# Far-half residual sums stored with 32-column blocks exchanged, and the far operands of the up projection read in one 128-partition transfer each

## The chip, the cores and the metric

The kernel runs on one core of one Trainium2 chip. Its time is the device time of one execution in microseconds (us); a median is taken over several runs. A profiled execution, taken by the hardware profiler, gives each instruction's start and duration. The engines are PE (matrix multiplications), DVE (vector), ACT (activations), POOL (a second element-wise engine) and SP, which computes nothing here and issues nearly all the transfers (DMAs) between DRAM and the on-chip memory, one after the other in a fixed order.

## The reference

One transformer layer on a sequence of 2048 tokens of width 1024: a layer norm, linear attention with a learned feature map (32 heads of width 32), an output projection `wo` with a residual, a second layer norm, and a dense layer of width 3584 with a relu, with a second residual. All in float32.

```python
x = A_x
h = x + _A_ref(_layernorm(x, axis=-1), A_wqkv, A_w_phi, A_wo)
h2 = h + _B_ref(_layernorm(h, axis=-1), B_w1, B_w2)
# _A_ref: q, k, v = x @ wqkv; phi = [softmax(p), softmax(-p)] with p = q @ w_phi (k alike)
#         o = phi_q (phi_k^T v) / (phi_q sum(phi_k)); o @ wo
# _B_ref: relu(x @ w1) @ w2
```

## The kernel before

**Staging.** PE runs matrix products from beginning to end: keys and values, queries, attention, the output projection (wo), the up projection (w1) and the down projection (w2). Each float32 operand is split into a high part, rounded to the form that PE takes, and the low remainder, and every product is three matmuls: high x high, high x low, low x high (`mm3`, L181 to L184). For a weight, ACT makes the high part (L125), and DVE or POOL subtracts it for the low part (L129); the weight's raw form comes by an SP transfer (L337) into a ring of six tiles called raw.

**Tokens and products.** The 2048 tokens are sixteen tiles of 128. Tiles 0 to 7 are the near half (b=0), tiles 8 to 15 the far half (b=1). In the up and down projections the operands are cut into 2 x 2 blocks and multiplied by a fast scheme with seven block products, m=1 to 7, in place of eight. The order of the seven in the up projection is UP = (1, 5, 6, 2, 7, 3, 4), with two column groups p of the weight in turn for each m: the up projection runs over b, then over pairs of p, then over m, then over the two p. Each m has an operand tile hT (named hT1 to hT7) of 128 partitions x 2 parts (high, low) x 4 x 512. The near half's operands stand in these tiles from the start of the up projection; when m's last product of the near half has run, the far half's operand of that m is loaded over it.

**From wo to the operands.** `wo_load` (L656 to L658) reads half a row block of x into one of four tiles called xh (128 x 512). When PE has the wo product of that half block in PSUM, `wo_add` (L683, L684) adds it on DVE, in place, giving the residual sum h. `wo_store` (L686, L687) writes h to DRAM, to hd. For a far tile `far_stats` (L735 to L741) takes the layer norm's statistics from the same tile. During the up projection of the near half, `far_pair` (L756 to L786) reads hd of a far tile back into xin, normalizes it on ACT, transposes it in blocks of 32 x 32 on DVE (L754), and forms the seven sums of the block scheme; `far_store` (L789 to L794) writes these to DRAM, to hs[1, m]. Here a block of 32 columns of the model width stands on 32 partitions: the transposes of 32 x 32 blocks leave, of the four blocks a and the four blocks c that make up 512 columns, a in the partitions and c in the columns, where the operand wants c in the partitions and a in the columns.

**The operand's load.** `h_load` (L798 to L808) reads hs[b, m] into the low part of hT[m], in two halves g=0 and 1. For b=0 it is two transfers of 256 KB (L804). For b=1 it is four transfers (L808), one for each q, of 32 partitions by 4 x 256 columns, 128 KB each: in these the blocks a and c change places. Then ACT copies it into the high part (`h_high`, L816), and DVE subtracts (`h_low`, L820). PE's matmuls read both.

**Down.** `d_load` (L903 to L907) reads h from hd again, `d_add` (L909, L910) adds the down product in PSUM, and `d_store` (L912 to L915) writes the output. One name (x1 to x4) is one quarter of a half's output, and takes one or two products in turn: the first `d_add` of a name is that of the m which also loads it.

**Order.** Nothing is scheduled by dependencies alone. The program counts PE's steps: a step is three matmuls, an item of wo is eight steps, an item of the up projection four. `do` (L189) and `when` (L971) set each piece of work beside one step, and each engine executes its instructions in the order in which the program was recorded. The tables that matter here: L1109 to L1118 put the load of a wo item, its add (nine steps after the item's start, eleven for the first two) and its store (fourteen steps after); L1143 to L1154 put `h_load`, `h_high` and `h_low`. For b=1 the load of m stands at the step behind m's last near product plus 2j + 3g, with j its place in UP (0 to 6) and g its half; `h_high` 22 + 4g and `h_low` 25 + 4g steps behind the step with g=0. L1177 to L1187 do the same for the down projection.

**SP's queue.** SP issues in program order, and what stands behind a waiting transfer waits too. The built program gives SP's transfers eight completion counters in turn, so each SP transfer also waits until the eighth transfer before it has landed: at most eight are in flight.

Of the kernel before, what the change touches and what calls it, by code (L numbers as in the profile page):

```python
# [9 lines left out]
F32 = mybir.dt.float32  # L10
# [5 lines left out]
P = 128  # L16
# [6 lines left out]
HT = NT // 2  # L23
# [26 lines left out]
BANK_OF = {6: 1, 7: 1, 4: 1, 3: 5}  # L50
# [90 lines left out]
def kernel(  # L141
# [12 lines left out]
    v, act, pool, pe, sp = nc.vector, nc.scalar, nc.gpsimd, nc.tensor, nc.sync  # L154
# [18 lines left out]
    def f32(ap):  # L173
        return ap.bitcast(F32)
# [14 lines left out]
    def do(n, k, f, *args):  # L189
        at[n, k].append((f, args))  # L190
# [11 lines left out]
    hs = {(b, m): dram.tile([P, 4, 4, P], F32, name=f"hs{b}_{m}") for b in range(2) for m in UP}  # L202
# [448 lines left out]
            v.tensor_sub(at_out(u, 1, g), at_in(ps), f32(at_out(u, 0, g)))  # L651

    oT, opool = {}, {}
    xh, wo_ps = {}, {}

    def wo_load(t, hf):  # L656
        xh[t, hf] = hp.tile([P, 512], F32, name="xh", bufs=4)
        sp.dma_start(xh[t, hf], x[t * P:(t + 1) * P, hf * 512:(hf + 1) * 512])  # L658

    def wo_item(t, hf, keys):  # L660
        b, i = place_of[t]
        o = oT[b]
        ps = wo_ps[t, hf] = mm_bank()
        for c in range(8):
            w = W.get(keys[c])
            mm3(ps, o[:, 0, c, i * P:(i + 1) * P], o[:, 1, c, i * P:(i + 1) * P], w[:, 0, :], w[:, 1, :],
                c == 0, c == 7)
            yield
# [12 lines left out]
            yield  # L681

    def wo_add(t, hf):  # L683
        v.tensor_add(xh[t, hf], wo_ps.pop((t, hf)), xh[t, hf])  # L684

    def wo_store(t, hf):  # L686
        sp.dma_start(hd[t][:, hf * 512:(hf + 1) * 512], xh.pop((t, hf)))  # L687
# [108 lines left out]
    sums, hT = {}, {}  # L796

    def h_load(b, m, g):  # L798

        cols = slice(2 * g * P, 2 * (g + 1) * P)  # L800
        if b == 0:
            lo = hT[m][:, 1, :, cols].rearrange("p k (i n) -> p k i n", i=2)
            for i in range(2):
                sp.dma_start(f32(lo[:, :, i, :]), hs[b, m][:, 2 * g + i])  # L804
            return
        src = hs[b, m].rearrange("(a k) q i n -> q k a (i n)", a=4)
        for q in range(4):
            sp.dma_start(f32(hT[m][32 * q:32 * (q + 1), 1, :, cols]), src[q, :, :, cols])  # L808

    def h_parts(m, g):  # L810

# [74 lines left out]
    dbank = {}  # L886
# [14 lines left out]
    d = {}  # L901

    def d_load(b, name, q):  # L903

        r, hf = {"x1": (0, 0), "x2": (0, 1), "x3": (1, 0), "x4": (1, 1)}[name]
        d[name, q] = t = dp.tile([P, 512], F32, name=f"{name}_{q}")
        sp.dma_start(t, hd[HT * b + 4 * r + q][:, hf * 512:(hf + 1) * 512])  # L907

    def d_add(b, m, name, q):  # L909
        v.tensor_add(d[name, q], dbank[b, BANK_OF.get(m, m)][q], d[name, q])  # L910

    def d_store(b, name, q):  # L912
        r, hf = {"x1": (0, 0), "x2": (0, 1), "x3": (1, 0), "x4": (1, 1)}[name]
# [6 lines left out]
    def item(gen, *args, keys):  # L920
        items.append((gen, args + (keys,)))
        steps.extend((k,) for k in keys)
        return len(items) - 1
# [10 lines left out]
    wo_first = len(items)  # L934
    for b, tiles in enumerate(groups):
        for hf in range(2):

            pairs = b == 0 and hf == 0
            for j in range(0, 4, 2 if pairs else 1):
# [3 lines left out]
                for half in range(2):  # L943
                    n = item(wo_pair, tiles[j:j + 2], hf, half, keys=[("wo", hf, 4 * half + k // 2) for k in range(8)])
# [26 lines left out]
    def when(step, f, *args):  # L971

        if step < 8 * first_up:
            do(step // 8, step % 8, f, *args)
        else:
            do(first_up + (step - 8 * first_up) // 4, step % 4, f, *args)
# [4 lines left out]
    for t in range(1, NT):  # L981
        n = t - 1 if t < HT else q_n[1, t - HT] + 1
# [125 lines left out]

    order = sorted(wo_n.items(), key=lambda kv: kv[1])  # L1109
    for (t, hf), n in order:  # L1110
        do(max(n - 1, wo_first), -1, wo_load, t, hf)
        added = 8 * n + (11 if n < wo_first + 2 else 9)
        when(added, wo_add, t, hf)
        if t >= HT:
            when(added, far_stats, t, hf)
            if hf == 1:
                when(added + 4, ln_power, ("f", t))
        when(8 * n + (10 if n > order[-3][1] else 14), wo_store, t, hf)  # L1118
# [24 lines left out]
    for j, m in enumerate(UP):  # L1143

        for g in range(2):
            step = up0 + (8 * j + (-62, -32)[g] if j < 4 else 6 * (j - 4) + 10 + 2 * g)
            high = up0 + (8 * j + (-48, -19)[g] if j < 4 else 6 * (j - 4) + 20 + 2 * g)
            when(step, h_load, 0, m, g)
            when(high, h_high, m, g)
            when(high + (2 if j < 4 else 5), h_low, m, g)  # L1150
            step = up_step(0, NP - 1, m) + 2 * j
            when(step + 3 * g, h_load, 1, m, g)
            when(step + 22 + 4 * g, h_high, m, g)
            when(step + 25 + 4 * g, h_low, m, g)  # L1154
# [22 lines left out]
    for b in range(2):  # L1177
        for m in DOWN:
            n = down_n[b, m, NP - 1] + 1
            name, more = {1: "x1", 5: "x4", 6: "x2", 4: "x3"}.get(m), \  # L1180
                {3: "x2", 7: "x4", 2: "x1", 4: "x3"}.get(m)
            for q in range(4):
                if name:
                    do(n - 8, q, d_load, b, name, q)
                do(n, q, d_add, b, m, name or more, q)
                if more:
                    do(n + 1, q, d_store, b, more, q)  # L1187

# [101 lines left out]
```

## Time and profile before

| quantity | value |
|---|---|
| runs | 1884.54, 1890.76, 1887.76 us; median 1887.76 us |
| profiled execution, its own time | 1886.22 us |
| its span (first to last instruction) | 1884.4 us |
| mean granted PE clock in it | 0.998 of full speed |
| bytes moved by DMA | 432.17 MB, 229 GB/s over the span |
| SP transfers called raw<-t (256 KB each) | 224, median 4.0 us from issue to landing |
| SP transfers called ad<-c (256 KB each) | 112, median 3.7 us |
| statistics of a far tile, 128 x 512, on DVE (L738) | 0.694 us |

A row of a timeline is: start, duration, engine, line, operation, out <- in, count; in brackets the idle time just ahead of it and the work whose end released it. A row of a window is, for each engine, busy time and the number of instructions, then the granted PE clock, the busy share of the sixteen DMA engines, and what they moved in GB/s. The chain of waits is followed back from the last instruction: each piece is what the next one waited for. The names in it: raw<-t and raw<-in_w_dram are raw weights loaded, ad<-c and ad<-s are results of the up projection stored, hT<-hs is `h_load`. SPq stands for SP's issuing of a transfer, PEld for PE's loading of weights, which runs beside its matmuls.

### The profile page before, as it was taken

What the parts mean: (1) busy time and instruction counts of PE and PEld (TensorE: products, weight loads), DVE (VectorE), ACT (ScalarE), POOL (GpSimd) and SP (SyncE); (2) the same over time, 40 slices, a digit from 0 to 9 for tenths busy, and PEclk for the clock granted to TensorE, in tenths of its full rate; (3) what the DMA queues carried; (4) which work ended last, traced back from release to release, by engine and by line L of the source; (5) the groups of instructions that cost most, each with busy time, mean ns of one, the idle gap of its engine ahead of it and who ended that gap; (6) DMA issues with size and microseconds to landing.
All of it is one profiled execution on the core that took longest, in us unless ns stands there. A gap on an engine that the chain in (4) does not pass through costs nothing.

```text
span 1884.4 us, 31901 instructions
## 1 busy us (share of the span) xinstructions
PE 1872.2 (99%) x11608; PEld 1535.5 (81%) x11608; DVE 1069.7 (57%) x1695; ACT 739.2 (39%) x1271; POOL 973.2 (52%) x959
## 2 busy tenths in 40 slices
PE   9999999999999999999999999999999999999999
PEld 7877788888787888888888878888888888888887
DVE  7787688677689777565555653344433433343333
ACT  5322245222233122355555544444444444444442
POOL 4887744888846988333333222222344444444443
PEclk9999999999999999999999999999999999999999
DMA  7888788656565666887888995666677677767775
GB/s 227 291 290 289 231 291 258 204 187 198 186 218 171 207 225 220 272 258 238 250 263 261 273 280 179 191 190 214 211 237 216 202 230 238 238 214 218 217 215 177
DMA packets 303949, 432.17 MB, mean 229 GB/s; under 512 B 24880, under 2 KB 166192, under 8 KB 303792
## 3 DMA queue, kind: packets, MB, share of 16 engines
q1 hardware_dynamic: 286896, 413.36, 70.6%
q10 hardware_dynamic: 16896, 16.78, 2.6%
q8 instruction: 91, 1.49, 0.3%
q14 instruction: 66, 0.54, 0.1%
HBM read 292.68 MB, written 137.36 MB: 228 GB/s over the span
## 4 chain that ended last, share of the span: by engine, by line
PE 96%; DMA 2%; POOL 1%; DVE 0%; ACT 0%; issue 0%; SPq 0%; POOLq 0%; ACTq 0%
PE mm L182 25%; PE mm L183 24%; PE mm L184 24%; PE ac L182 4%; PE ac L184 4%; PE ac L183 4%; PE tp L184 2%; PE tp L183 2%; PE tp L182 2%; PE tp L245 1%; PE ac L464 1%; PE tp L633 1%; DMA raw<-t 1%; PE ac L633 1%; POOL w L129 0%; DMA ad<-c 0%
## 5 line engine op out<-in xcount | busy, mean ns | idle before, releaser
L129 POOL TENSOR_TENSOR w<-raw,w 128x512 fp32r<-128x512 f32 x353 | 470.4, 1334 | 727.7 <-ACT w L125 666.4
L125 ACT ACTIVATE w<-raw 128x512 fp32r<-128x512 f32 x686 | 409.0, 626 | 507.9 <-PE mm L184 240.8
L129 DVE TENSOR_TENSOR w<-raw,w 128x512 fp32r<-128x512 f32 x333 | 272.7, 820 | 520.3 <-ACT w L125 516.9
L182 PE MATMUL mm<-w,xT 128*128 128x512 f32 x768 | 305.4, 398 | 0.0
L183 PE MATMUL mm<-w,xT 128*128 128x512 f32 x768 | 299.9, 390 | 0.7 <-POOL w L400 0.4
L184 PE MATMUL mm<-w,xT 128*128 128x512 f32 x768 | 299.3, 390 | 0.0
L183 PE MATMUL mm<-hT,w 128*128 128x512 f32 x672 | 262.3, 390 | 2.2 <-DMA ad<-c 2.2
L182 PE MATMUL mm<-hT,w 128*128 128x512 f32 x672 | 262.5, 391 | 2.0 <-DMA raw<-in_w_dram 2.0
L184 PE MATMUL mm<-hT,w 128*128 128x512 f32 x672 | 262.1, 390 | 0.0
L182 PEld LDWEIGHTS mm<-w,xT 128*128 128x128 f32 x768 | 144.2, 188 | 34.0 <-issue 2.9
L362 POOL TENSOR_TENSOR b<-b 128x256 f32<-128x256 f32 x176 | 143.5, 816 | 52.9 <-DMA b<-in_w_dram 35.6
L184 PEld LDWEIGHTS mm<-w,xT 128*128 128x128 f32 x768 | 144.2, 188 | 30.6
L183 PEld LDWEIGHTS mm<-w,xT 128*128 128x128 f32 x768 | 144.3, 188 | 29.9 <-POOL w L129 1.0
L182 PE MATMUL mm<-w 128*128 128x512 f32 x392 | 152.5, 389 | 0.0
L183 PE MATMUL mm<-w 128*128 128x512 f32 x392 | 152.5, 389 | 0.0
L184 PE MATMUL mm<-w 128*128 128x512 f32 x392 | 152.5, 389 | 0.0
L183 PEld LDWEIGHTS mm<-hT,w 128*128 128x128 f32 x672 | 126.7, 188 | 29.1 <-DVE hT L820 2.7
L182 PEld LDWEIGHTS mm<-hT,w 128*128 128x128 f32 x672 | 126.7, 188 | 28.8 <-ACT hT L816 2.4
L184 PEld LDWEIGHTS mm<-hT,w 128*128 128x128 f32 x672 | 126.6, 188 | 26.1
L183 PEld LDWEIGHTS mm<-w 128*128 128x128 f32 x392 | 73.6, 188 | 15.3
L182 PEld LDWEIGHTS mm<-w 128*128 128x128 f32 x392 | 73.6, 188 | 15.3
L184 PEld LDWEIGHTS mm<-w 128*128 128x128 f32 x392 | 73.6, 188 | 15.3
(180 smaller groups left out, 3143.6 us busy)
## 6 DMA issues: line engine op xcount, KB each, us to landing
raw<-t SPq DMA_DIRECT2D x224, 256.0 KB, 4.0
raw<-ad SPq DMA_DIRECT2D x196, 256.0 KB, 3.0
raw<-in_w_dram SPq DMA_DIRECT2D x168, 256.0 KB, 3.1
ad<-c SPq DMA_DIRECT2D x112, 256.0 KB, 3.7
b<-in_w_dram SPq DMA_DIRECT2D x44, 512.0 KB, 5.7
t<-b SPq DMA_DIRECT2D x44, 512.0 KB, 4.4
ad<-s SPq DMA_DIRECT2D x84, 256.0 KB, 4.1
ed<-qe ACTq DMA_DIRECT2D x32, 512.0 KB, 4.5
```

Of the source, the lines that this page charges most:

```text
L125: nc.scalar.activation(w[:, 0, :], raw[1], AF.Copy)
L129: eng.tensor_tensor(out=w[:, 1, :], in0=raw[1], in1=w[:, 0, :].bitcast(F32), op=ALU.subtract)
L182: pe.matmul(ps, a_hi, b_hi, start=first, stop=False, skip_group_check=more)
L183: pe.matmul(ps, a_hi, b_lo, start=False, stop=False, skip_group_check=more)
L184: pe.matmul(ps, a_lo, b_hi, start=False, stop=last, skip_group_check=more)
L245: pe.transpose(pt[:, k, :], xn[:, (4 * j + k) * P:(4 * j + k + 1) * P], ident)
L362: pool.tensor_tensor(out=tsum[*u, *out], in0=tsum[*u, *a], in1=tsum[*u, *b], op=ALU.subtract)
L464: pe.matmul(kv_ps[s][g][32 * i:32 * (i + 1), 0:64], vt[:, 32 * h:32 * (h + 1)], phi[:, 64 * h:64 * (h + 1)], start=first, stop=last)
L633: pe.matmul(banks[g][32 * c:32 * (c + 1), j * P:(j + 1) * P], kvL[rows, 4 * q + 2 * sd + h // 4, 32 * (h % 4):32 * (h % 4 + 1)], phT_of[u ...
```

## The change

There are three parts.

1. *The layout of far h.* `wo_add` of a far tile writes its sum with the 4 x 4 blocks of 32 columns exchanged inside each 512 columns (`mixed`), into a second xh tile, so each far half block takes two of the four xh tiles and no longer one. `far_stats` and `wo_store` use that tile. The load of a far half block's x is recorded five steps ahead of its wo item (two steps for the second far one), where it was eight steps ahead.
2. *The operand's load.* `h_load` of b=1 is one transfer of 128 partitions x 4 x 256 (512 KB) for each m and g, where it was four of 32 partitions x 4 x 256 (128 KB each): 14 issues in place of 56. Its step is the same.
3. *The last residual.* hd of the far half now holds exchanged columns, so `d_load` of b=1 reads into one of twelve tiles called dl, and the first `d_add` of a name reads that tile through `mixed` and writes a new tile in the plain order.

```diff
     def wo_load(t, hf):
         xh[t, hf] = hp.tile([P, 512], F32, name="xh", bufs=4)
         sp.dma_start(xh[t, hf], x[t * P:(t + 1) * P, hf * 512:(hf + 1) * 512])
+        if t >= HT:
+            xg[t, hf] = hp.tile([P, 512], F32, name="xh", bufs=4)
...
     def wo_add(t, hf):
-        v.tensor_add(xh[t, hf], wo_ps.pop((t, hf)), xh[t, hf])
+        ps, h = wo_ps.pop((t, hf)), xh[t, hf]
+        if t < HT:
+            v.tensor_add(h, ps, h)
+            return
+        xh[t, hf] = y = xg.pop((t, hf))
+        v.tensor_add(mixed(y), ps.rearrange("p (c a k) -> p c a k", c=4, a=4),
+                     h.rearrange("p (c a k) -> p c a k", c=4, a=4))
+
+    def mixed(y):
+        return y.rearrange("p (a c k) -> p c a k", a=4, c=4)
...
-        src = hs[b, m].rearrange("(a k) q i n -> q k a (i n)", a=4)
-        for q in range(4):
-            sp.dma_start(f32(hT[m][32 * q:32 * (q + 1), 1, :, cols]), src[q, :, :, cols])
+        sp.dma_start(f32(hT[m][:, 1, :, cols]), hs[b, m].rearrange("p k i n -> p k (i n)")[:, :, cols])
...
-        d[name, q] = t = dp.tile([P, 512], F32, name=f"{name}_{q}")
+        d[name, q] = t = dp.tile([P, 512], F32, name=f"{name}_{q}") if b == 0 else \
+            dp.tile([P, 512], F32, name="dl", bufs=12)
...
-    def d_add(b, m, name, q):
-        v.tensor_add(d[name, q], dbank[b, BANK_OF.get(m, m)][q], d[name, q])
+    def d_add(b, m, name, q, first):
+        ps, h = dbank[b, BANK_OF.get(m, m)][q], d[name, q]
+        if b == 0 or not first:
+            v.tensor_add(h, ps, h)
+            return
+        d[name, q] = y = dp.tile([P, 512], F32, name=f"{name}_{q}")
+        v.tensor_add(y.rearrange("p (c a k) -> p c a k", c=4, a=4),
+                     ps.rearrange("p (c a k) -> p c a k", c=4, a=4), mixed(h))
...
-        do(max(n - 1, wo_first), -1, wo_load, t, hf)
+        if t < HT:
+            do(max(n - 1, wo_first), -1, wo_load, t, hf)
+            last_near = n
+        else:
+            when(8 * n - (2 if n == last_near + 2 else 5), wo_load, t, hf)
```

DVE, ACT and PE keep the order of their instructions. SP has 42 transfers fewer, 1417 in place of 1459; the lines of the changed kernel are a few higher (L658 stays, L684 is L691, L687 is L698, L808 is L817, L820 is L829, L858 is L867).

Three places show what moves. The first is SP late in the up projection of the near half, at the far operand of m=7 (hs_7 is its sums in DRAM). Before:

```order
L858 DMA ad_4_13_211<-c_11697 128x512
L337 DMA raw<-t_0_310 128x512
L858 DMA ad_2_12_168<-c_11720 128x512
L337 DMA raw<-t_1_311 128x512
L808 DMA hT_9621<-hs_7_111 32x4x256 x8
L858 DMA ad_2_13_169<-c_11744 128x512
L337 DMA raw<-in_w_dram 128x512
L858 DMA ad_5_12_140<-s_11923 128x512
```

Of the change, at the same place:

```order
L867 DMA ad_4_13_211<-c_11707 128x512
L337 DMA raw<-t_0_310 128x512
L867 DMA ad_2_12_168<-c_11727 128x512
L337 DMA raw<-t_1_311 128x512
L817 DMA hT_9637<-hs_7_111 128x4x256 x2
L867 DMA ad_2_13_169<-c_11748 128x512
L337 DMA raw<-in_w_dram 128x512
L867 DMA ad_5_12_140<-s_11909 128x512
```

Eight issues have become two, at the same place between the same neighbours. The same holds for each of the seven m.

The second place is SP near the end of the wo stage, around the load of the far half block that is item 28 of 32 (counted from 0). Its x comes by the row `xh<-in_x_dram`; the waits are in brackets, DMAHW0 to 7 being the eight completion counters. Before:

```order
L687 DMA hd_97<-xh 128x512 [waits DVE_49]
L658 DMA xh<-in_x_dram 128x512 [waits DMAHW6_49,DMAHW1_49]
L337 DMA raw<-in_w_dram 128x512 [waits DMAHW7_49,Pool_49]
L804 DMA hT_9199<-hs_2_103 128x4x128 [waits DMAHW0_49]
L804 DMA hT_9199<-hs_2_103 128x4x128
L733 DMA hs_1_100<-xin 128x512 [waits DMAHW2_49]
```

Of the change:

```order
L698 DMA hd_97<-xh 128x512 [waits DMAHW5_49,DVE_49]
L337 DMA raw<-in_w_dram 128x512 [waits DMAHW6_49,Pool_49]
L815 DMA hT_9208<-hs_2_103 128x4x128 [waits DMAHW7_49]
L815 DMA hT_9208<-hs_2_103 128x4x128 [waits DMAHW0_49]
L658 DMA xh<-in_x_dram 128x512 [waits DMAHW5_49,DVE_49]
L744 DMA hs_1_100<-xin 128x512 [waits DMAHW2_49]
```

The load of x has moved behind the load of a raw weight, which waits for POOL, and behind two operand loads.

The third place is DVE at the same item's add, with the statistics and an `h_low` behind it. Before:

```order
L684 TENSOR_TENSOR xh_9371<-mm_9425,xh_9371 128x512 [waits DMAHW6_49,DMAHW1_49,PE_49]
L738 BN_STATS hst_9281<-xh_9371 128x6 [waits DVE_49]
L741 BN_AGGR mv_9487<-hst_9281 128x2 [waits DVE_49,Pool_49]
L820 TENSOR_TENSOR hT2_9199<-hT2_9199 128x4x256 [waits DMAHW1_49,DMAHW0_49,Activation_49]
L129 TENSOR_TENSOR w_9499<-raw_9220,w_9499 128x512 [waits Activation_49]
```

Of the change:

```order
L691 TENSOR_TENSOR xh_9410<-mm_9436,xh_9408 128x4x4x32 [waits DMAHW7_49,DMAHW1_49,PE_49]
L749 BN_STATS hst_9289<-xh_9410 128x6 [waits DVE_49]
L752 BN_AGGR mv_9499<-hst_9289 128x2 [waits DVE_49,Pool_49]
L829 TENSOR_TENSOR hT2_9208<-hT2_9208 128x4x256 [waits DMAHW0_49,Activation_49]
L129 TENSOR_TENSOR w_9514<-raw_9227,w_9514 128x512 [waits Activation_49]
```

The add reads one tile (xh_9408) and writes another (xh_9410), and the counter DMAHW7 that it now waits on is that of the store two half blocks back, hd_98<-xh, which read the tile that the add writes.

More of the change, by code (lines that the diff above doesn't have):

```diff
@@ L653 @@
     oT, opool = {}, {}
-    xh, wo_ps = {}, {}
+    xh, xg, wo_ps = {}, {}, {}
     def wo_load(t, hf):
@@ L1184 @@
                     do(n - 8, q, d_load, b, name, q)
-                do(n, q, d_add, b, m, name or more, q)
+                do(n, q, d_add, b, m, name or more, q, name is not None)
                 if more:
```

## The prediction, made before the changed kernel ran

> **What bounds the kernel now.** I read the page first, the busy shares of the engines (the span is 1884.4 us).
>
> ```profile
> PE 1872.2 (99%) x11608; PEld 1535.5 (81%) x11608; DVE 1069.7 (57%) x1695; ACT 739.2 (39%) x1271; POOL 973.2 (52%) x959
> ```
>
> PE is busy 99% of the span, so only a hole in PE's work can be won or lost. The second view is PE's list of waits from 820 us (the end of the wo stage) to the end, which has two rows:
>
> ```profile
> PE mm L183 <- DMA ad<-c: 2.2, 1, 2.2
> PE mm L182 <- DMA raw<-in_w_dram: 2.0, 1, 2.0
> ```
>
> The third is PE's timeline around them:
>
> ```profile
> 1073.88 0.39 PE L182 MATMUL mm<-hT,w 128*128 128x512 f32 x1
> ...
> 1097.68 0.39 PE L182 MATMUL mm<-hT,w 128*128 128x512 f32 x1
> ...
> 1106.29 0.39 PE L184 MATMUL mm<-hT,w 128*128 128x512 f32 x1
> 1108.64 0.79 PE L182 MATMUL mm<-hT,w 128*128 128x512 f32 x1 [1.96 <-DMA raw<-in_w_dram]
> 1111.62 0.79 PE L183 MATMUL mm<-hT,w 128*128 128x512 f32 x1 [2.19 <-DMA ad<-c]
> ...
> 1116.05 0.40 PE L182 MATMUL mm<-hT,w 128*128 128x512 f32 x1
> ```
>
> From 1097.68 to 1106.29 there are 38 intervals between matmuls, 0.2266 us each; that is the undisturbed pitch. From 1106.29 to 1116.05 there are 13 intervals in 9.76 us; undisturbed they take 13 x 0.2266 = 2.95. **6.81 us are lost here**: 1.96 + 2.19 = 4.15 idle, and 2.66 because the matmuls behind the idle times come slower (L182 and L183 take 0.79 in place of 0.39). The windows below show the granted clock at 0.79 over 1104 to 1120, and 1.00 on both sides.
>
> The first of these matmuls is the first of m=4 for the far half, the last of the seven to change over. The releasers that the view names had been done before; the operand is what came last (one row each of SP's, ACT's and DVE's timeline):
>
> ```profile
> 1095.10 8.24 SPq L808 DMA_DIRECT2D hT<-hs  x8
> 1107.53 1.06 ACT L816 ACTIVATE hT<-hT 128x1024 fp32r<-128x1024 f32 x1 [1.09 <-DMA hT<-hs]
> 1110.35 1.21 DVE L820 TENSOR_TENSOR hT<-hT 128x1024 fp32r<-128x1024 f32 x1
> ```
>
> The eight loads of m=4 are issued over 8.24 us to 1103.34; ACT's `h_high` waits for the last and ends at 1108.59, when L182 (high x high) starts; DVE's `h_low` ends at 1111.56, when L183 starts. Why the loads are so late is in the chain of waits from 1070 to 1108, its shares by line and its last transfers:
>
> ```profile
> by line: DMA raw<-t 33.7%; DMA ad<-c 23.5%; DMA hT<-hs 20.4%; DMA ad<-s 11.5%; PE mm L183 4.8%; PE mm L182 4.8%; PE mm L184 4.4%; ACT w L125 1.6%; ACT c L849 1.4%; SPq L858 1.2%; SPq L337 1.1%; issue 1.1%
> ...
> 1094.54 8.48 DMA raw<-t
> 1103.02 0.02 issue
> 1103.04 2.24 DMA hT<-hs
> ```
>
> 89% of it are transfers, one behind the other with no engine between: each starts about 0.02 us after an earlier one has landed, the eighth before it by the counters. SP is bound by eight transfers in flight, hence by their number and landing time:
>
> ```profile
> L808 SPq DMA_DIRECT2D hT<-hs x56: 302/372/1469, 1044.1 to 1103.0; - x56
> DMA to landing us min/median/max: 3.9/5.3/8.2
> ```
>
> From the first L808 to the last, SP's order has 85 transfers, in 58.9 us: 0.693 us each, about an eighth of the landing time (5.3 / 8 = 0.66).
>
> **The load in one piece.** The same stretch of SP's order is now 43 transfers, 14 of them operand loads. A far load is 128 x 4 x 256, 512 KB in runs of 1 KB. The trace has another line of that size and form:
>
> ```profile
> L352 SPq DMA_DIRECT2D b<-in_w_dram x44: 368/436/2692, 28.3 to 503.7; - x44
> DMA to landing us min/median/max: 3.9/5.8/10.8
> ```
>
> It lands in 5.8 us at the median, hardly more than 128 KB before. 43 x 5.8 / 8 = 31 us, from 1044 to 1075, so SP keeps up with the program and no longer sets the time. Then the loads of m=4 are issued where they are recorded: its tile is free at 1073.88 (first matmul of the far half, 144 matmuls ahead of m=4's), the loads stand 12 and 15 steps behind that. A step is 3 x 0.2266 = 0.68 us, so they go out at 1082.1 and 1084.1 and land by 1090 (1095 at the longest). `h_high` and `h_low` of g=1 stand 38 and 41 steps behind 1073.88; `h_low` then starts at 1101.8 and ends 1.2 later, at 1103.0, while the matmul is due at 1106.52. The margin is 3.5 us, so the whole stall goes: **-6.81 us**. At the other end, every transfer takes 10.8 us: 43 x 10.8 / 8 = 58 us, as late as now, and the gain is zero. I take the median, since the stores and raw weights in between are of an unchanged form.
>
> Can the transfers carry it? The windows:
>
> ```profile
> 1040.00:1044.00 4.00, 4.00 (x20) 3.30 (x19) 2.73 (x3) 1.12 (x2) 0.88 (x1) 1.00 1.03 368
> 1044.00:1104.00 60.00, 60.00 (x266) 49.70 (x265) 34.66 (x39) 34.49 (x52) 15.11 (x10) 1.00 1.03 267
> 1104.00:1120.00 16.00, 11.85 (x42) 8.93 (x41) 8.06 (x10) 8.68 (x14) 4.34 (x3) 0.79 0.86 260
> 1120.00:1200.00 80.00, 80.00 (x355) 66.24 (x354) 34.80 (x48) 34.33 (x59) 19.66 (x15) 1.00 0.62 197
> ```
>
> The last three columns are clock, DMA share and GB/s. The same full share, 1.03, moved 368 GB/s just ahead of the loads and 267 while they ran: packets into 32 partitions hold the DMA engines longer. The stage without the loads needs 197 GB/s; the loads are 14 x 0.524 MB = 7.34 MB, 122 GB/s over 60 us. Together 320, under the 368.
>
> (The Trainium skill, page "SBUF — State Buffer", section "Door 1: The DMA port swizzle (why `[64,N]` ≈ `[32,N]`)", says why: 32 neighbouring partitions reach 8 of the 16 ports, and only a transfer over all 128 reaches every one. Here the trace shows a fall to 267 / 368 = 0.73 in a mixture, not to a half. By the rule a transfer over all partitions would land in less time than four over 32, which leaves the sum as it is.)
>
> **The wo stage pays.** A far half block takes two of the four xh tiles, and its x is asked for later. The place where this comes near PE is the end of the stage:
>
> ```profile
> 775.73 0.35 SPq L658 DMA_DIRECT2D xh<-in_x_dram  x1
> 783.71 0.33 SPq L337 DMA_DIRECT2D raw<-in_w_dram  x1
> ...
> 788.32 0.91 SPq L687 DMA_DIRECT2D hd<-xh  x1
> 790.33 0.69 DVE L684 TENSOR_TENSOR xh<-mm,xh 128x512 f32<-128x512 f32 x1 [2.30 <-PE mm L184]
> 800.54 1.23 DVE L820 TENSOR_TENSOR hT<-hT 128x1024 fp32r<-128x1024 f32 x1 [5.64 <-ACT hT L816]
> 826.40 2.35 DVE L820 TENSOR_TENSOR hT<-hT 128x1024 fp32r<-128x1024 f32 x2
> 829.05 0.39 PE L182 MATMUL mm<-hT,w 128*128 128x512 f32 x1
> ```
>
> Before, SP sends the load of item 28's x at 775.73 and then waits for POOL to free a raw tile until 783.71. After, that load stands behind the raw weight, so it falls into the crowded stretch that follows, where SP catches up. All behind it, the near operands (L804) too, come one place later; a place costs an eighth of a landing, about the 0.69 us found above. The operand of m=7 ends at 828.75 (826.40 + 2.35), and its first matmul starts at 829.05: 0.30 us of margin. So PE loses **+0.4 us**: none if `h_high` and `h_low`, which stand at fixed steps, take up the delay, 0.7 if several loads pile up.
>
> The second cost is on DVE. Item 28's add must now wait until the store at 788.32 (L687) has landed; the landing times of that line's 32 stores:
>
> ```profile
> DMA to landing us min/median/max: 2.0/4.7/9.0
> ```
>
> 788.32 + 4.7 = 793.0, 2.7 us later than 790.33; with the longest, 9.0, it is 797.3, 7.0 later. Behind it on DVE stand the statistics, an `h_low` and a weight's split, and then DVE idles 5.64 us ahead of 800.54, which covers the median. PE has four mm banks of 5.44 us (eight steps) each, so a late add does not hold it. I take **0**. What it costs without that cover is a rival.
>
> **The exchanged forms cost nothing.** On DVE the nearest rows are a subtraction whose output is scattered over columns and one without that:
>
> ```profile
> L651 DVE TENSOR_TENSOR oT<-tp,oT x32: 354/408/425, 554.8 to 761.0; 128x256 fp32r<-128x256 f32 x32
> L179 DVE TENSOR_TENSOR w<-mm,w 128x256 fp32r<-128x256 f32 x4 | 1.6, 411 | 1.1 <-ACT w L178 1.1
> ```
>
> 408 ns against 411, equal. DVE is at 57%, so in the stages a longer add would be hidden; only the last four adds of the program (x3, added and stored at once by m=4) stand on the path that ends last, and for them I allow 0 to 0.5 us. That the new dl tiles take room ahead of earlier tiles' release has no row; the loads stand eight items ahead of their adds, so I put it within the same 0.5.
>
> **Sum**, on the profiled execution's own time: 1886.22 - 6.81 + 0.4 + 0 = 1879.8, with its own range 1879.4 to 1881.0 from the bounds of the added costs. That execution lies 1.54 us below the median. If the difference lies elsewhere, the median moves to 1881.4; if it is the size of this very stall, which may differ between runs, the result is 1879.8. I take the middle, **1880.6 us**, 0.38% less; the own range is 1878 to 1883, which allows a run-to-run difference of some 2 us around.
>
> (The Trainium skill, page "TensorE: Matmul & The Clock Gate", section "HAM oscillation — how this bites in real kernels", puts the limit for an idle PE at about 3.4 us before the clock falls. The trace differs: two gaps of 1.96 and 2.19 us, and a clock of 0.79. By the rule a new short gap at 829 costs itself alone; by the trace it can cost 6.81 / 4.15 = 1.64 times itself, 0.7 instead of 0.4.)
>
> **Rivals.**
>
> *R1, the large loads land slowly.* 43 transfers at landing times towards 10.8 us would again bind SP, and m=4 comes in time only in part. For it: the largest landing, and that a transfer of four times the size holds its counter longer. Against: the median 5.8 under a load like this. With half of the stall left, 1886.2 - 3.4 + 0.4, and half of the 1.54: 1884.0 us.
>
> *R2, the wo stage loses more than the far half wins.* The mechanism is DVE's add that waits for the store two half blocks back, while SP itself is held up by POOL (the 7.98 us between 775.73 and 783.71): the adds, the `h_low` behind them and so m=7's first matmul come late. If the 5.64 us of idle DVE do not cover it, the delay is 2.7 + 0.69 to 7.0 + 0.69; less the margin of 0.30 and times 1.64 for the slow clock, PE loses 5.1 to 12.1 us at m=7, and half as much again if m=3, which follows through the same queue, is late too: 1886.2 - 6.8 + 5.1 = 1884.5 to 1886.2 - 6.8 + 18.2 = 1897.6, about 1891 in the middle. Nothing is won any more from a delay of 0.30 + 6.81 / 1.64 = 4.5 us. For it: the new counter in the add's row, the margin of 0.30. Against: the idle time and the fixed steps.
>
> *R3, it doesn't do what it says.* The stall comes from the one long landing (raw<-t, 8.48 us, at 1094.54), from the traffic of weights and stores, and the same bytes bring it back: 1886.2 + 0.4 + 1.5 = 1888.1. Against it: each of the pieces of the chain ahead of it is a landing too, and SP would have been ten microseconds ahead by then.
>
> **How the numbers follow.** Forecast 0.58, R1 0.15, R2 0.20, R3 0.07. About 0.3%, 5.7 us, can be told from no change: faster is below 1882.1, slower above 1893.4. Of the forecast 0.52 is faster and 0.06 no change (its range reaches 1883). R1 gives 0.05 faster and 0.10 no change. R2 gives 0.10 no change and 0.10 slower, its upper half. R3 gives 0.06 and 0.01. Faster 0.57, same 0.32, slower 0.11. The range begins at 1877.5, since two more microseconds may lie in the runs' difference, and ends at 1888.5, which takes in R1 and R3 and leaves out the most of R2.
>
> **What would show it.** Right: no wait of PE between 1100 and 1120, clock 1.00 there; the operand loads of m=4 issued at 1082 to 1085, SP waiting for the program and not for landings; windows of 1044 to 1104 at over 300 GB/s with a share under 1; a PE gap of under 1 us at 829. Wrong: landing times of the large loads near 10 us (R1); DVE's add of item 28 at 793 or later with PE gaps near 829 or earlier in the wo stage (R2); a stall again at 1106 though SP is not late (R3). A stall at another changeover of the far half would mean that the loads now take a place that raw weights need.

## The result, and the profile after

| | median | range | runs |
|---|---|---|---|
| before | 1887.75 us | 1882.55 to 1890.76 | 12 |
| changed | 1882.67 us | 1880.58 to 1883.67 | 12 |

The ratio is 0.9975, with a 95% interval of 0.9966 to 0.9985: 5.1 us or 0.25% less. The changed kernel is faster beyond the uncertainty of this comparison, though by less than the 0.3% that the prediction had put down as the limit of what can be told. The prediction was 1880.6 us.

The profiled execution of the changed kernel took 1883.67 us, its span is 1881.9 us. Its list of waits of PE from 820 us to the end has one row, where there were two:

```profile
PE mm L183 <- DVE hT L829: 2.8, 1, 2.8
```

The windows of the late up projection of the near half (busy time and count for PE, PEld, DVE, ACT and POOL, then clock, DMA share, GB/s), and the far operand's loads:

```profile
1044.00:1104.00 60.00, 60.00 (x267) 49.67 (x266) 38.34 (x44) 36.82 (x57) 16.59 (x11) 1.00 0.95 324
1104.00:1120.00 16.00, 16.00 (x72) 13.27 (x71) 10.29 (x14) 8.43 (x15) 4.41 (x3) 1.00 0.65 194
```

```profile
L817 SPq DMA_DIRECT2D hT<-hs x14: 524/530/810, 1048.8 to 1091.5; - x14
...
DMA to landing us min/median/max: 5.5/7.0/8.6
```

PE runs through at a clock of 1.00 where it lost 6.81 us; the same operands come at 324 GB/s instead of 267, with a DMA share of 0.95 instead of 1.03. The old hole is gone.

A new one has opened where the prediction had put 0.4 us, at the first matmul of m=7 for the near half. PE's timeline there:

```profile
828.80 0.39 PE L182 MATMUL mm<-hT,w 128*128 128x512 f32 x1
832.03 0.50 PE L183 MATMUL mm<-hT,w 128*128 128x512 f32 x1 [2.84 <-DVE hT L829]
...
832.67 0.63 PE L182 MATMUL mm<-hT,w 128*128 128x512 f32 x1
833.09 0.63 PE L183 MATMUL mm<-hT,w 128*128 128x512 f32 x1
...
836.24 0.39 PE L182 MATMUL mm<-hT,w 128*128 128x512 f32 x1
```

From 828.80 to 836.24 there are 12 intervals in 7.44 us; at the undisturbed 0.2266 they take 2.72. So 4.7 us are lost, 2.84 of them idle and the rest to slower matmuls (0.42 from 832.67 to 833.09). What is late there, from SP's timeline, DVE's, and SP's again:

```profile
788.70 0.82 SPq L698 DMA_DIRECT2D hd<-xh  x1
```

```profile
796.20 0.69 DVE L691 TENSOR_TENSOR xh<-mm,xh 128x512 f32<-128x512 f32 x1 [8.41 <-DMA hd<-xh]
...
829.62 2.35 DVE L829 TENSOR_TENSOR hT<-hT 128x1024 fp32r<-128x1024 f32 x2
```

```profile
798.85 0.37 SPq L337 DMA_DIRECT2D raw<-in_w_dram  x1
...
803.21 0.33 SPq L337 DMA_DIRECT2D raw<-in_w_dram  x1
...
818.43 0.93 SPq L815 DMA_DIRECT2D hT<-hs  x2
...
819.96 0.98 SPq L815 DMA_DIRECT2D hT<-hs  x2
```

The same of SP before the change:

```profile
798.60 1.18 SPq L337 DMA_DIRECT2D raw<-in_w_dram  x2
...
816.06 0.94 SPq L804 DMA_DIRECT2D hT<-hs  x2
...
817.60 0.97 SPq L804 DMA_DIRECT2D hT<-hs  x2
```

DVE's add of item 28 waits for the landing of the store that was issued at 788.70; it runs at 796.20, where it ran at 790.33. SP sends the second of two raw weights at 803.21; before, both were out by 799.8 (two in 1.18 us from 798.60). The operand loads of m=7 (the last two rows of both views) stand behind that in SP's queue. On the way the lateness is handed on between the engines: SP asks for the x of item 31 at 806.20 instead of 801.34, its add runs at 811.98 instead of 810.46, and DVE's subtraction that frees the tile of a raw weight ahead of m=7's loads runs at 817.30 instead of 814.94. So these loads go out 2.4 us later, and their `h_low` ends at 831.97 instead of 828.75.

Without their holes the two profiled executions are alike: 1886.22 - 6.81 = 1879.4 and 1883.67 - 4.7 = 1879.0. The kernel with early stores and raw tiles in turn, below, which has neither hole, took 1879.24 in its profile. Against some 1879.2, and if nothing else differs from run to run, the median before stands for holes of 8.5 us in all, and that of the changed kernel for 3.5: an estimate, since most runs have no profile.

### The profile page after: what moved, and what is told of

Read it like the earlier page. It is cut to its first block, busy times and chain, and to the rows that moved or that the text cites. A ratio compares the mean times of both kernels' runs of the same rounds, so it can differ in the third digit from the quotient of the medians.

```text
span 1881.9 us, 31799 instructions
## 1 busy us (share of the span) xinstructions
PE 1871.4 (99%) x11608; PEld 1535.3 (82%) x11608; DVE 1070.6 (57%) x1695; ACT 739.0 (39%) x1271; POOL 973.1 (52%) x959
## 4 chain that ended last, share of the span: by engine, by line
PE 95%; DMA 2%; POOL 1%; DVE 1%; issue 0%; ACT 0%; SPq 0%; DVEq 0%; ACTq 0%; POOLq 0%
PE mm L182 25%; PE mm L183 24%; PE mm L184 24%; PE ac L183 4%; PE ac L182 4%; PE ac L184 4%; PE tp L183 2%; PE tp L184 2%; PE tp L182 2%; PE tp L245 1%; PE ac L464 1%; PE tp L633 1%; DMA hT<-hs 1%; DMA hs<-xin 1%; PE ac L633 1%; POOL w L129 0%
```

## The experiments

In all of them PE computes the same matmuls in the same order. The kernel before was run beside each group; its medians were 1886.44, 1886.89 and 1886.37 us.

**The first part alone.** In the kernel before, far sums go into a second tile and far x comes later, but the layout and the loads stay:

```diff
+        xh[t, hf] = y = xg.pop((t, hf))
+        v.tensor_add(y, ps, h)
...
+            when(8 * n - (2 if n == last_near + 2 else 5), wo_load, t, hf)
```

> The kernel before with the first part of the change alone: far sums go into a second xh tile and far x is loaded later, but the sums keep their plain layout, and the far operands are read in four transfers of 32 partitions as before. Theory: the new hole of the changed kernel at 829 us (4.6 us: 2.8 idle, the rest slow clock) belongs to this part alone, and the old hole at 1106 us (6.8 us) stays unless PE's delay gives the loads time: two holes, 4 to 5 us at 829 and 4 to 7 us at 1107, and a time of 1889 to 1893 us, 0.1 to 0.3% over before. Rival (the hole at 829 comes from the exchanged form of the add or from the later stages): one hole at 1107 us and a time equal to before.

Measured: 1889.29 us beside 1886.44, ratio 1.0011 (0.9999 to 1.0023). The waits of PE from 820 us in its profile:

```profile
PE mm L183 <- DMA raw<-in_w_dram: 2.5, 1, 2.5
PE mm L183 <- DVE hT L827: 0.9, 1, 0.9
PE mm L182 <- DMA raw<-in_w_dram: 0.2, 1, 0.2
```

There are two holes, as the theory says, so a hole at 829 us comes with this part and needs neither the exchanged form nor the loads. Both are smaller in this profile than foreseen (0.9 us idle at 829, 2.7 at 1107); the profiled execution was the shortest of its twelve (1883.39 us; the others reach 1892.73). The median's 2.9 us is not told from zero by its interval, which reaches 0.23%, 4.3 us.

**The form of the far loads.** Three kernels keep all else of the change and cut the one transfer of 512 KB in different ways: four of 32 partitions, four of 128 partitions by 256 columns, two of 64 neighbouring partitions.

```diff
+        for q in range(4):
+            sp.dma_start(f32(hT[m][32 * q:32 * (q + 1), 1, :, cols]), src[32 * q:32 * (q + 1), :, cols])
```

```diff
+        for k in range(4):
+            sp.dma_start(f32(hT[m][:, 1, k, cols]), src[:, k, cols])
```

```diff
+        for q in range(2):
+            sp.dma_start(f32(hT[m][64 * q:64 * (q + 1), 1, :, cols]), src[64 * q:64 * (q + 1), :, cols])
```

> The changed kernel with each far operand read again in four transfers of 32 partitions, 128 KB each (56 issues), from the exchanged layout. Theory (number of transfers in SP's eight counters, or their narrowness): the hole at 1107 us comes back with 4 to 7 us beside that at 829 us, 1887 to 1890 us. Rival (the hole at 1107 belonged to the order of the blocks or to the run, not to the loads' form): no hole at 1107 us, time as the changed kernel, 1882 to 1883.5 us.

> The changed kernel with each far operand read in four transfers of 128 partitions by 256 columns, 128 KB each: 56 issues as in the kernel before, but over all partitions. Told apart from the narrow form of the same count. If the count of transfers against the eight counters is what binds SP: the hole at 1107 us is back, 4 to 7 us, landing times near 5 us, 1887 to 1890 us. Rival (the spread over partitions is what helps): landing times fall to 4 us or less, SP is not late, no hole at 1107 us, 1882 to 1884 us.

> The changed kernel with each far operand read in two transfers of 64 neighbouring partitions, 256 KB each (28 issues). If the spread over partitions counts and 64 neighbours reach as little as 32: landing times well over those of 128 partitions for the same bytes (6 us or more), windows of 1044 to 1104 us at a full DMA share and under 290 GB/s, and a hole at 1107 us of 2 to 6 us; 1884 to 1889 us. If half of the spread is enough, or the number of transfers: landing 5 us or less, over 300 GB/s, no hole at 1107 us, 1881.5 to 1883 us.

Measured, with the changed kernel's first profile for comparison:

| form | transfers | median us | ratio to before (95%) | landing, median us | GB/s and DMA share, 1044 to 1104 |
|---|---|---|---|---|---|
| 4 x 32 partitions | 56 | 1890.48 | 1.0021 (1.0012 to 1.0029) | 5.1 | 260, 0.99 |
| 2 x 64 partitions | 28 | 1885.47 | 0.9995 (0.9985 to 1.0005) | 7.4 | 282, 1.08 |
| 4 x 128 partitions | 56 | 1881.99 | 0.9974 (0.9964 to 0.9983) | 4.0 | 296, 0.92 |
| 1 x 128 partitions | 14 | 1882.67 | 0.9975 (0.9966 to 0.9985) | 7.0 | 324, 0.95 |

The last row is the changed kernel's result from above, taken beside its own runs of the kernel before.

The rows for the two forms with 56 transfers, first 32 partitions and then 128, each with its PE waits from 820 us:

```profile
L819 SPq DMA_DIRECT2D hT<-hs x56: 538/594/1276, 1045.7 to 1106.4; - x56
...
DMA to landing us min/median/max: 3.3/5.1/6.9
```

```profile
PE mm L183 <- DMA raw<-in_w_dram: 3.2, 1, 3.2
PE mm L182 <- DMA raw<-in_w_dram: 2.6, 1, 2.6
PE mm L183 <- DVE hT L831: 2.0, 2, 1.4
```

```profile
L819 SPq DMA_DIRECT2D hT<-hs x56: 319/405/1357, 1046.4 to 1098.3; - x56
...
DMA to landing us min/median/max: 2.9/4.0/6.2
```

```profile
PE mm L183 <- DVE hT L831: 1.6, 1, 1.6
```

With as many transfers of the same size as before, spread over all partitions, the hole at 1107 us does not come back; with 32 partitions it does, and is larger than expected (8.3 us from 1108.54 to 1119.56, of them 5.8 idle). The time that SP needs to issue a load does not explain it: with 32 partitions in the kernel before it was 0.372 us at the median, less than the 0.405 with 128 partitions here, and that kernel has the hole. So what the change has won in the far half is the spread over partitions, and the smaller number of transfers is not needed for it. The two kernels, alike in the number and size of the transfers, are 8.5 us apart (1890.48 and 1881.99). Two transfers of 64 partitions are in between: the landing of 256 KB takes longer than that of 512 KB over 128, the DMA share is full again, and PE waits 1.11 us at 1109 us in this profile, less than the 2 to 6 us expected. The profiled execution took 1882.84 us; its other runs reach 1889.78, so the hole may well be larger in most of them; there is no profile of those.

The Trainium skill, page "SBUF — State Buffer", section "Door 1: The DMA port swizzle (why `[64,N]` ≈ `[32,N]`)", has the first 64 partitions reach the same ports as the first 32. The landing times agree: 7.4 us for 64 partitions' 256 KB against 4.0 for 128 partitions' 128 KB and 7.0 for their 512 KB.

**The store earlier.** In the changed kernel, the store of each far half block is recorded one step behind its add instead of five (the last two stood there already), first for all of them, then only from item 26 on:

```diff
-        when(8 * n + (10 if n > order[-3][1] else 14), wo_store, t, hf)
+        when(8 * n + (10 if n > order[-3][1] or t >= HT else 14), wo_store, t, hf)
```

```diff
-        when(8 * n + (10 if n > order[-3][1] else 14), wo_store, t, hf)
+        when(8 * n + (10 if n > order[-7][1] else 14), wo_store, t, hf)
```

> The changed kernel with the store of every far half block recorded one step behind its add instead of five. Theory (the hole at 829 us comes from DVE's add of item 28, which waits until 796 us for the store two half blocks back): that store goes out at 785 to 786 us instead of 788.7, lands by 792, the add of item 28 runs at 791 to 792, and the hole at 829 us shrinks from 4.6 us to under 2 us; 1879 to 1881 us. Rival (the hole comes from SP being late by the place of the x loads, whatever DVE does): the hole stays at 4 us or grows, since the stores now stand ahead of the operand loads; 1882 to 1885 us.

> The changed kernel with the early store (one step behind the add) only for the last far half blocks, from item 26 on, so that no store is moved ahead of the near half's loads before 783 us. Theory: item 28's add runs at 790 to 792 us instead of 796, PE's loss of 2 us at 776 us that came with all stores early is gone, and the hole at 829 us is under 1.5 us: 1880 to 1882 us. Rival (any store that is moved ahead costs the operand loads behind it what it saves): hole at 829 us of 1.5 to 3 us, 1882 to 1883.5 us.

Measured: 1883.06 us (ratio 0.9985, 0.9976 to 0.9993) with all stores early, 1880.72 us (0.9970, 0.9959 to 0.9980) with the last six. With all early, 1879 to 1881 us was missed. The add of item 28 no longer waits for the store: it runs 15.0 us ahead of the first up matmul, where it ran 16.1 ahead before the change and 10.0 in the changed kernel. But a transpose at 778 us waits 2.00 us, with slow matmuls behind it, and at m=7's first product, now at 833 us, 1.3 us of idle time stay. With the last six, the rows of PE's waits from 820 us and of DVE's add:

```profile
PE mm L183 <- DVE hT L829: 1.3, 1, 1.3
```

```profile
791.46 0.69 DVE L691 TENSOR_TENSOR xh<-mm,xh 128x512 f32<-128x512 f32 x1 [3.69 <-DMA xh<-in_x_dram]
```

The add runs 4.7 us earlier than in the changed kernel, since its store goes out at 783.86 and lands in 3.2 us, and still 1.3 us of idle PE remain. The wait on the store is not all of the hole.

**One tile again.** DVE adds x onto the product in PSUM, ACT writes the exchanged blocks into the tile that held x, and x comes as early as before:

```diff
+        v.tensor_add(ps, ps, h)
+        act.activation(mixed(h), ps.rearrange("p (c a k) -> p c a k", c=4, a=4), AF.Copy)
+        xg[t, hf] = ps
```

> The changed kernel with one xh tile for each far half block again: DVE adds x onto the product in PSUM, ACT writes the exchanged blocks from PSUM into the tile that held x (some 0.6 us of ACT each, 16 of them), the statistics are read from PSUM, and the x loads stand eight steps ahead as before the change. Theory (the hole at 829 us comes from the second tile: the add's wait for the store two half blocks back and the later x loads): item 28's add runs at 790 to 791 us, the hole at 829 us is under 0.5 us, no hole at 1107 us, 1878 to 1880 us. Rival (the hole comes from DVE's exchanged form, from the place of SP's raw loads or from a fresh ACT load): a hole of 1.5 to 4.6 us at 829 us stays, 1881 to 1884 us.

Measured: 1882.01 us (0.9977, 0.9968 to 0.9986). PE has no wait from 820 us on, which bears the theory out: without the second tile the hole at 829 us goes. PE comes 3.45 us later to the up projection (first matmul at 809.66, 806.21 in the changed kernel), but this delay is not what closes the hole: measured from that matmul, the add of item 28 (16.1 us ahead) and the last operand load of m=7 (11.6 us behind) are where they were before the change. The time is no better than the changed kernel's, since PE now waits 1.17 and 1.31 us for ACT at two transposes near 740 us, where ACT has the new copies to do; 1878 to 1880 us was wrong.

**The raw tiles in turn.** What remained with the early stores is found in SP's waits. In the kernel before, the second raw weight at item 29 takes the tile that DVE's subtraction frees, and the next one that POOL's frees. With the second xh tile these two have changed places in the built program: the ring hands out tiles in the order in which they come free as the program is built, and there DVE's subtraction now falls behind POOL's. Why it does so is not shown; with the early stores the order is the same, since SP still waits 2.1 us for POOL there and sends this load at 802.67. In the changed kernel it stands still for POOL until 803.19, when this subtraction ends:

```profile
801.38 1.81 POOL L129 TENSOR_TENSOR w<-raw,w 128x512 fp32r<-128x512 f32 x1 [0.93 <-ACT w L125]
```

An edit gives each of the six raw tiles its own name, so that they go strictly in turn:

```diff
-        self.held.append([False, self.pool.tile(self.shape, self.dtype, name=self.name)])
+        self.held.append([False, self.pool.tile(self.shape, self.dtype, name=f"raw{len(self.held) % RR}" if self.name == "raw" else self.name, bufs=1 if self.name == "raw" else self.bufs)])
```

> The changed kernel with the six raw tiles taken strictly in turn, so that the raw weight behind item 29's x load takes the tile that DVE frees (as in the kernel before) and not the one that POOL frees later. In the changed kernel that load waits for POOL until 3.0 us ahead of the first up matmul, where it went out 7.0 us ahead in the kernel before. Theory (two causes: DVE's add waits for the store two back, and the raw tiles have changed places): the raw load goes out earlier by 1 us or more, but the add is still late, so the hole at 829 us shrinks and stays: 1 to 2 us idle, 1880.5 to 1882.5 us. Rival A (the raw tile is all of it): hole under 0.5 us, 1879 to 1880 us. Rival B (only the add's wait counts): hole as in the changed kernel, 1882 to 1883.5 us.

> Both cures together: early stores from item 26 on, and the raw tiles in turn. Theory (the two causes add up): the last operand load of m=7 goes out 11.6 us behind the first up matmul, as in the kernel before (14.2 in the changed kernel, 12.5 with early stores alone), no hole at 829 us over 0.5 us and none at 1107 us, 1878.5 to 1879.8 us. Rival (a third cause, such as the place of the x loads): a hole of 1 to 1.5 us stays, 1880 to 1881 us.

> The changed kernel unaltered, beside the two cures on the same chip, for a second profile of its hole at 829 us. Theory (the hole is set by one late chain and the clock comes down only in some runs): 2 to 5 us lost there, 1881 to 1883.5 us, and no hole at 1107 us. Rival (the hole in its first profile was a rare event): under 1 us, 1879 to 1880.5 us.

| kernel | median us | range | ratio to before (95%) | idle PE at 829 us |
|---|---|---|---|---|
| changed, again | 1881.75 | 1880.60 to 1883.64 | 0.9976 (0.9967 to 0.9985) | 1.5 |
| raw tiles in turn | 1880.08 | 1879.05 to 1880.78 | 0.9964 (0.9950 to 0.9977) | 1.4 |
| late stores early, raw tiles in turn | 1879.61 | 1879.18 to 1880.87 | 0.9964 (0.9952 to 0.9977) | 0 |

The same raw load (L337, at 803.21 in the changed kernel) and DVE's add of item 28, with the raw tiles in turn alone:

```profile
800.38 0.33 SPq L337 DMA_DIRECT2D raw<-in_w_dram  x1
```

```profile
796.21 0.69 DVE L691 TENSOR_TENSOR xh<-mm,xh 128x512 f32<-128x512 f32 x1 [8.28 <-DMA hs<-s4l]
```

The load goes out 2.8 us earlier, with the add as late as ever, and the hole stays at 1.4 us, so rival A is out. Rival B is out by the median, 1.7 us below that of the changed kernel beside it (the expected 1880.5 was just undercut), but not by the idle time: the changed kernel's second profile has 1.5 us, hardly more than either edit alone (1.4 and 1.3). With both edits, DVE's `h_low` of m=7 is in time:

```profile
791.62 0.69 DVE L691 TENSOR_TENSOR xh<-mm,xh 128x512 f32<-128x512 f32 x1 [3.61 <-DMA xh<-in_x_dram]
...
826.74 2.35 DVE L829 TENSOR_TENSOR hT<-hT 128x1024 fp32r<-128x1024 f32 x2
```

It ends at 829.09, and the matmul that reads it follows at 829.25 without a wait; the list of PE's waits from 820 us is empty. Its last operand load is issued 11.7 us behind the first up matmul, against 11.6 before the change, 14.2 and 13.1 in the two profiles of the changed kernel, and 12.5 and 12.3 with the stores or the raw tiles alone. So each edit brings these loads forward, and only the two together close the hole, in one profile of each kernel. This kernel beats both: its median is 6.8 us under that of the kernel before and 2.1 under the changed kernel's in the same group.

The changed kernel's second profile has the late chain too, with 1.5 us idle, 1.8 us lost (2 to 5 were expected) and a clock of 1.00, where the first had 2.84 idle and a clock of 0.57 over 832 to 836. Its runs fall into two groups in both sets of measurements (1880.6 to 1881.8, and 1882.5 to 1883.7), about as far apart as these two profiles (1880.80 and 1883.67 us). The mean granted clock is 1.000 in all eleven runs of the faster group and 0.999 in ten of the twelve of the other, as in the two profiles: so the slower group is the one in which the clock comes down.

## Why the prediction was right, and where it was not

- *What bounds the kernel now.* Right: the hole at 1107 us was what could be won, and it was won. It seems to make the runs differ too: the runs of kernels with far loads over 32 or 64 partitions lie 4.0 to 9.8 us apart (lowest to highest of 11 to 34 runs), those with 128 partitions 1.7 to 4.6 us (5 to 12 runs).
- *The load in one piece, -6.81 us.* The size is right for the profiled execution. Against the median it was rather too small: by the estimate above the median before stands for some 1.5 us more of holes, which is the 1.54 that the prediction had left undecided and split in half.
- *Its reason.* In part wrong. The prediction put the number of transfers (43 in place of 85) into the sum and the spread over partitions into the check of the rates. The runs show that the landing time of narrow transfers is what counts: 85 transfers with 4.0 us of landing pass through the same stretch in time. That the gain came out right with the count as its ground is in part luck: this change lowers the count and widens the loads at once. The landing time taken from L352, 5.8 us, was too short for 512 KB in this stage (7.0), and the loads of m=4 went out 12.5 us behind the first far matmul (1090.89 from 1078.37) instead of 8.2. SP's longest wait over 1040 to 1108 is now for POOL to free raw tiles (third view below; 0.5 us before the change), but of this only 2.0 us fall between 1076 and 1092, beside waits of 0.2 to 1.1 us for DVE, ACT and landings, so POOL is one cause of several:

```profile
1078.37 0.39 PE L182 MATMUL mm<-hT,w 128*128 128x512 f32 x1
...
1111.01 0.39 PE L182 MATMUL mm<-hT,w 128*128 128x512 f32 x1
```

```profile
1107.69 1.22 DVE L829 TENSOR_TENSOR hT<-hT 128x1024 fp32r<-128x1024 f32 x1
```

```profile
SPq L337 <- POOL w L129: 19.1, 10, 3.0
```

  Of the margin of 3.5 us that was foreseen, 2.1 were left (1108.91 to 1111.01). It sufficed.
- *The rates.* Right: 324 GB/s at a share under 1, where 320 had been worked out.
- *The wo stage pays, +0.4 us and 0.* This is the step that failed, and by its size, not its place. The place of the hole, m=7's first matmul, and both late things ahead of it, SP's raw weights and DVE's add behind the store, are in the prediction; what they cost is 4.7 us in the first profile, 1.5 of idle time in the second, and some 3.5 in the median. The add was put at 793.0 (the store's landing at the median, 4.7); it ran at 795.4 to 796.2, since that store took 6.4 and 7.4 us in the two profiles. The trace before had the landing of this very store, 5.9 us, and the median of all 32 hid it. The 5.64 us of idle DVE behind the add were taken for full cover. They covered the `h_low` at 800.54; that the weight's subtraction between the two also frees a raw tile for SP was left out. And a tile's change of place in the ring, which brought POOL into SP's way, was not seen at all.
- *The exchanged forms.* Right: far adds of 128 x 4 x 4 x 32 take 0.69 us, like the plain ones, and so do the last adds of the program:

```profile
1877.57 1.37 DVE L925 TENSOR_TENSOR x<-ac,dl 128x512 f32<-128x512 f32 x2
```

- *The sum.* 2.1 us too low: about 3 too little for the wo stage, against 1 too little for the far half's gain. That the one partly makes up for the other is luck. The upper end of the sum's own range, 1881.0, needs the slow clock (1.64 x 0.7 + 0.5); the bounds as they are stated, 0.7 and 0.5, give 1880.6.
- *The rivals.* R1 is out, since the landing times stayed at 5.5 to 8.6 us; R3 is out, since the same bytes bring no hole. R2 had the right mechanism: DVE's add at 793 or later with a PE gap near 829, its sign, is what came, and the sign of the forecast, a gap under 1 us there, did not. Its price at m=7 began at 5.1 us, and 4.7 was measured in the first profile; m=3 behind it was not late, and the far half's gain was larger.
- *The clock.* The multiple of 1.64 for an idle time fits the first profile (4.7 / 2.84 = 1.66), and not the second, where 1.5 us of idle time cost 1.8 in all and left the clock at 1.00.

## What to carry to other kernels

Ask of a transfer how many partitions it reaches before asking how many transfers there are: a layout that is exchanged where it is produced, at no cost to the engine that writes it, let the load reach all 128. When a tile gets a second buffer out of a pool of fixed size, the buffer's reuse is a new wait on the store that reads it; follow that wait to everything queued behind it, and to which engine frees the tiles of other rings. If a ring's order matters, name its tiles, so that an edit elsewhere cannot change it. And for a wait on one transfer, take the landing of that very transfer from the trace, not the median of its line.

## What the runs showed of the hardware beyond what was expected

The clock does not follow from the length of an idle time of PE alone. An idle time of 1.3 to 1.7 us brought no lower clock in any profile, nor did 2.23 us near the start of the program (one tile again, idle up to 9.00 us; clock 1.00 over 8 to 12). With 2.00 us at 778 us (all stores early) the clock was 0.68 over 780 to 784, with 2.84 us at 829 us it was 0.57 over 832 to 836; but 2.48 us at 1108 us (the first part alone) cost two matmuls of 0.50 us and no more. What tells these apart was not tried. The Trainium skill, page "TensorE: Matmul & The Clock Gate", section "HAM oscillation — how this bites in real kernels", has the limit at some 3.4 us of idle time; the first two of these are below it and were slowed all the same.

Four transfers of 32 partitions from rows that stand together in DRAM were no better than the old ones, which gathered every fourth row: landing 5.1 against 5.3 us, but 0.594 us to issue against 0.372. Why the issue takes longer stays open.
